# Sliding-window attention and SwiGLU: unit 7's attention-value products and x ahead of unit 8's transpositions and scores in the source

## The chip, the cores and the metric

The kernel runs on one core of a Trainium2 chip. The metric is the device time of one execution in microseconds. A core has five engines with a queue each: TensorE (PE in the profile, with its weight loads as PEld) multiplies matrices, VectorE (DVE) and ScalarE (ACT) do the elementwise work and read TensorE's results from PSUM, GpSimd (POOL) issues the loads here, and SyncE (SP) issues transposing DMAs and the stores.

## The reference

Attention with a causal window of 128 keys and a linear bias per head, over 8 batches, 8 heads, 576 positions and head dimension 64. Its output, as 4608 tokens by 512, is the input of a gated feed-forward network (FFN) with 1536 hidden columns.

```python
scores = scale * np.matmul(q, k.transpose(0, 1, 3, 2))
bias = slopes[:, None, None] * (-np.abs(rel))[None, :, :]
mask = (rel >= 0) & (rel < window)            # window = 128
scores = np.where(mask, scores + bias[None], -1e9)
attn = softmax(scores)                        # over the keys
attn_out = np.matmul(attn, v)

x = attn_out.transpose(0, 2, 1, 3).reshape(B * S, H * D)
g = x @ w_gate
silu = g * (1.0 / (1.0 + np.exp(-g)))
out = (silu * (x @ w_val)) @ w_out
```

## The kernel before

**Units of attention.** A unit is 128 query rows with all 8 heads. Two batches make nine units (`units`, `p` from 0 to 8): four of the first batch, four of the second, and one combined unit (`p == 8`) that holds the last 64 rows of both. There are 36 units. Unit 8 is the first combined one. A unit needs: its k and q transposed (`transposed`, line 198: four products by an identity into the tile `pt`, copied out by ACT for k and by DVE for q; from rank 11 on a transposing DMA on SP in place of it), scores (`scores`, line 243; products `ps` at line 278 or, for units with 128 keys, `psc` at line 313, both with 64 rows of the array per head), the exponentials on ACT (lines 284 and 317, into `ex` and `exc`), the mask on DVE (lines 290 and 321), the attention-value products `av` (`weighted`, line 325, products at line 345, then a reciprocal and `x` on DVE), and x transposed (`x_transposed`, line 358: four products into `px`, copied to `xT` by ACT). Scores of a combined unit are three sets of 128 keys; for unit 8 all three are made at once (`first + together(...)`).

**FFN.** Blocks of 512 tokens. Block 0 takes units 0 to 3, block 1 units 4 to 7, and so on; block 8 takes the combined units. A block makes, for 12 groups of 128 hidden columns, a gate product `pg` and a value product `pv` (line 397, four products each; ACT's tanh into `tt`, DVE's `uu` at line 416 and `hT` at line 427), and then the output product: `project` (line 446, `po` at line 451, twelve products) for block 0, and seven products in place of eight (`strassen`, line 504, products at line 532) for the others, for which DVE makes sums of weights (`weight_sums`, T at lines 475 to 478) and of `hT` (lines 485 to 488).

**Order.** `attention` (line 838) and `ffn` are generators. `everything` (line 937) walks through the FFN's steps, and after each pulls as many steps of the attention as a target says (`n_att < target`), or until the unit that the next block needs is done (`done < ready[blk]`, `ready[1]` being 8). For a unit `i`, `attention` first emits the transpositions and the scores of unit `i + 1`, one yield per step of these, then `weighted(i)`, a yield, `loads_to(i + 7)` and `ahead(i)`, a yield, `x_transposed(i)` and two yields. The value that it yields becomes `done`. What stands in the source is not yet the order on the engines: up to step 60 of the FFN a scheduler arranges TensorE, DVE and ACT from its own estimates, with the source's order as priority; from step 60 on (`FIXED_FROM`) TensorE's order is the source's, while DVE and ACT are still arranged. POOL's loads stand in the source's order throughout.

**Memory for products.** PSUM has 8 banks. The pool `ps_a` (tag "a") has 4, shared by `ps`, `psc`, `pt`, `av`, `px` and the strassen product `p`. The tag "gv" has 3, for `pg` and `pv`. The tag "po" has 1.

Of the kernel before, what the change touches and what calls it, by code (L numbers as in the profile page):

```python
# [39 lines left out]
def slot(h):  # L40

    return 4 * (h // 4) + 2 * (h % 2) + (h % 4) // 2
# [9 lines left out]
def kernel(  # L52
# [141 lines left out]
    def load(rank):  # L194
        load_qk(rank)
        load_v(rank)
# [34 lines left out]
    need = [18 * s + n for s in range(NSUP) for n in (3, 5, 7, 8, 11, 13, 15, 18 if s else 16, 18)]  # L231

    def transpose(n):
        name, rank = order[n]
        if rank < QK_DMA_FROM:
            transposed(name, rank)
            return
        t_ = (natk if name == "k" else natq).pop(rank)
        nc.sync.dma_start_transpose(transposed_home(name, rank), t_.rearrange("p h d -> p (h d)"))
# [3 lines left out]
    def scores(i):  # L243

        s, p = units[i]
        def combined(n):
            return scores_128(s, (3, 7, 8)[n], 8, (s, "c", n), msk[n])

        def together(one, two):
            return [one[0] + two[0]] + one[1:] + two[1:]  # L250

        if p == 8:
            first = combined(0) if s == 0 else []
            return first + together(combined(1), combined(2))
        if p == 7 and s == 0:
            return scores_128(s, p, p, (s, p), reg[:, :, 0:P])
        if p == 7:
            return together(scores_128(s, p, p, (s, p), reg[:, :, 0:P]), combined(0))
        if p == 3:
            return scores_128(s, p, p, (s, p), reg[:, :, 0:P], i < FIRST)  # L260
        ks = (9 * s + p) % NK
        banks = []
        early_tile = i < FIRST
        e = epool.tile([P, H, 256], FP16, name="ex", tag="ex", bufs=4)
        ex[(s, p)] = e

        def products():
            for q4 in range(2):
                two = [ps_a.tile([P, 2, 256], FP32, name="ps", tag="a") for _ in range(2)]
                banks.append(two)  # L270
                for par in range(2 if early_tile else 0):
                    o = 4 * q4 + 2 * par
                    nc.tensor.matmul(two[par], idm, bias[:, o:o + 2, :], start=True, stop=False)
                for j in range(2):
                    pair = 2 * q4 + j
                    for par in range(2):
                        rows = slice(64 * par, 64 * par + 64)
                        nc.tensor.matmul(two[par][:, j, :], kT[rows, ks, pair, :],  # L278
                                         qT[rows, p:p + 2, pair, :], start=(j == 0 and not early_tile),
                                         stop=(j == 1))  # L280

        def act(q4, par):
            o = 4 * q4 + 2 * par
            nc.scalar.activation(e[:, o:o + 2, :], banks[q4][par], AF.Exp, scale=scale)  # L284

        def mul(q4):
            if early_tile:
                return
            o = slice(4 * q4, 4 * q4 + 4)
            nc.vector.tensor_mul(e[:, o, :], e[:, o, :], reg[:, o, :])  # L290

        return [[products], [lambda: act(0, 0)], [lambda: act(0, 1), lambda: mul(0)],
                [lambda: act(1, 0)], [lambda: act(1, 1), lambda: mul(1)]]
# [31 lines left out]
    def weighted(i):  # L325

        s, p = units[i]
        x = xpool.tile([P, H, D], FP16, name="x", tag="x")
        xs[i] = x
        for half in range(2):  # L330
            pool, tag = (ps_f, "gv") if i < FIRST else (ps_a, "a")
            av = pool.tile([P, 4, D + 1], FP32, name="av", tag=tag)
            todo = []
            for j in range(4):
                h = 4 * half + j
                if p == 8:
                    for n, kt in enumerate((3, 7, 8)):
                        todo.append((j, ex[(s, "c", n)][:, slot(h), :], va[9 * s + kt][:, h, :]))
                else:
                    if p not in (0, 4):  # L340
                        todo.append((j, ex[(s, p - 1)][:, slot(h), 128:256],
                                     va[9 * s + p - 1][:, h, :]))
                    todo.append((j, ex[(s, p)][:, slot(h), 0:128], va[9 * s + p][:, h, :]))
            for n, (j, w, val) in enumerate(todo):
                nc.tensor.matmul(av[:, j, :], w, val, start=(n == 0), stop=(n == len(todo) - 1))  # L345
            rec = xpool.tile([P, 4, 1], FP32, name="rec", tag="rec", bufs=4)
            nc.vector.reciprocal(rec, av[:, :, D:D + 1])
            nc.vector.tensor_mul(x[:, 4 * half:4 * half + 4, :], av[:, :, 0:D],  # L348
                                 rec.broadcast_to([P, 4, D]))
# [3 lines left out]
    def place(i):  # L353

        s, p = units[i]
        return (8, s) if p == 8 else (2 * s + p // 4, p % 4)

    def x_transposed(i):
        n, j = place(i)
        if n not in xT:  # L360
            xT[n] = bpool.tile([P, NKB, 512], FP16, name="xT", tag="xTc" if n == 8 else "xT",
                               bufs=1 if n == 8 else 3)
        x = xs.pop(i).rearrange("p h d -> p (h d)")
        dst = xT[n][:, :, j * P:(j + 1) * P]
        if i >= X_DMA_FROM:
            nc.sync.dma_start_transpose(dst, x)
            return
        pool, tag, n = (ps_f, "po", 1) if i < FIRST else (ps_a, "a", 4)
        pt = pool.tile([P, NKB, P], FP16, name="px", tag=tag, bufs=n)
        for kb in range(NKB):  # L370
            nc.tensor.transpose(pt[:, kb, :], x[:, kb * P:(kb + 1) * P], idm if i < FIRST else idm2)  # L371
        if i < FIRST:
            nc.vector.tensor_copy(dst, pt)  # L373
        else:
            nc.scalar.copy(dst, pt)
# [404 lines left out]
    def loads_to(r):  # L780
        nonlocal loaded
        while loaded <= min(r, NR - 1):
            load(loaded)
            loaded += 1

    def transposes_to(n):
        nonlocal done_t
        while done_t < n:
            transpose(done_t)
            done_t += 1  # L790

    def ahead(i):

        n = need[min(i + 4, last)]
        while done_t < n and order[done_t][1] < loaded and order[done_t][1] >= QK_DMA_FROM:
            transposes_to(done_t + 1)

    def run(steps):
        for fs in steps:
            for f in fs:  # L800
                f()
            yield
# [35 lines left out]
    def attention():  # L838

        waiting = []  # L840
        transposes_to(need[FIRST])
        for _ in run(scores(FIRST)):
            yield FIRST
        for i in range(FIRST, last + 1):
            late = i >= LATE
            if i < last:
                transposes_to(need[i + 1])
                for n, _ in enumerate(run(scores(i + 1))):
                    yield i - len(waiting)
                    if n == 2 and late:  # L850
                        weighted(i)
                        yield i - len(waiting)
            if not late or i == last:
                weighted(i)
                yield i
            loads_to(i + 7)
            ahead(i)
            yield i - len(waiting)
            if late and i < X_DMA_FROM:
                if waiting:  # L860
                    x_transposed(waiting.pop(0))
                waiting.append(i)
                yield i
                yield i
                continue
            while waiting:
                x_transposed(waiting.pop(0))
            x_transposed(i)
            yield i
            yield i + 1  # L870
# [40 lines left out]


    att = attention()
    done = n_att = 0
    ready = [4, 8, 13, 17, 22, 26, 31, 35, 36]
# [90 lines left out]
```

## Time and profile before

| | us |
|---|---|
| median of 4 runs (lowest to highest) | 343.99 (343.88 to 344.37) |
| the profiled execution's own time | 343.88 |
| its span, first to last instruction | 342.1 |
| TensorE busy | 329.5 |
| DVE busy | 277.1 |
| ACT busy | 207.0 |
| POOL busy | 109.6 |

The granted TensorE clock is 1.00 in every stretch. By stretch, busy time (us) of TensorE, DVE and ACT:

| stretch | TensorE | DVE | ACT |
|---|---|---|---|
| 40 to 50 | 9.37 | 8.47 | 7.14 |
| 50 to 60 | 9.57 | 6.49 | 6.86 |
| 60 to 70 | 9.98 | 9.78 | 5.03 |
| 70 to 80 | 9.92 | 9.89 | 7.13 |
| 80 to 90 | 9.76 | 9.88 | 5.53 |
| 90 to 100 | 9.34 | 7.75 | 6.34 |
| 200 to 243 | 42.94 | 42.93 | 22.77 |

The span is counted from the first instruction to the last; the time of a run lies a little above it. In an order of time, a line gives the start, the length, the engine, the source line, the operation, output<-input, the shape, how many instructions of that kind follow one another (xN), and in brackets the idle time before it with what ended it. Matmuls are pipelined, so the length of one is longer than the distance to the next: what a product costs is read from one start to the next. The shape "64*128" marks products with 64 rows of the array.

### The profile page before, as it was taken

Reading aid. Unit: us, or ns where it says so; the run is one execution under the profiler, and the core shown is the slowest. Engines: PE = TensorE matmul, PEld = TensorE weight load, DVE = VectorE, ACT = ScalarE, POOL = GpSimd, SP = SyncE. Lnnn points to the kernel's source line nnn. Section 1 sums busy time; section 2 is a strip of 40 time slices with the busy share of each in tenths; the row PEclk is TensorE's granted clock in tenths of the full one; section 3 lists DMA queues with packets and bytes.
Section 4 is the critical chain, followed back from the end, with each engine's and each line's share of the span. In section 5 each row is a group of like instructions: output and inputs, shape, how many; then the busy total and the mean of one; then the engine's idle time right before and its main releaser. Section 6 shows DMA issues by size and latency. Waiting matters only on the chain.

```text
span 342.1 us, 7786 instructions
## 1 busy us (share of the span) xinstructions
PE 329.5 (96%) x2983; PEld 218.2 (64%) x2983; DVE 277.1 (81%) x652; ACT 207.0 (61%) x412; POOL 109.6 (32%) x136
## 2 busy tenths in 40 slices
PE   7999989999999999999999999999999999999995
PEld 3484445444456565565655655666788878888884
DVE  5577886999798769998899999999855975775683
ACT  3758676465666665666655647563477667676640
POOL 8977662648865176833017000000000000000000
PEclk9999999999999999999999999999999999999999
DMA  9999999999999999999949912041101101011014
GB/s 151 167 180 177 166 175 147 82 144 153 158 173 151 161 155 181 162 158 139 193 111 104 176 31 79 15 72 38 63 6 57 63 0 64 19 45 63 0 71 116
DMA packets 160037, 37.37 MB, mean 109 GB/s; under 512 B 147328, under 2 KB 155648, under 8 KB 160000
## 3 DMA queue, kind: packets, MB, share of 16 engines
q0 software_dynamic: 118336, 18.62, 82.1%
q1 hardware_dynamic: 40976, 17.64, 27.1%
q10 hardware_dynamic: 688, 0.62, 0.6%
q8 instruction: 23, 0.38, 0.5%
q14 instruction: 14, 0.11, 0.1%
HBM read 37.91 MB, written 9.44 MB: 138 GB/s over the span
## 4 chain that ended last, share of the span: by engine, by line
PE 75%; DVE 14%; ACT 6%; issue 3%; DMA 1%; ACTq 0%; DVEq 0%
PE po L532 16%; PE pg L397 14%; PE pv L397 14%; PE gX L624 8%; PE av L345 4%; PE gY L624 4%; PE ps L278 3%; PE p L532 2%; PE po L451 2%; DVE hT L427 2%; PE gZ L624 2%; ACT tt L415 2%; ACT ex L284 2%; DVE uu L416 2%; PE px L371 1%
## 5 line engine op out<-in xcount | busy, mean ns | idle before, releaser
L397 PE MATMUL pv<-xT,wv_sb 128*128 128x512 f16 (+2 forms) x320 | 76.5, 358 | 0.6 <-DVE uu L416 0.3
L397 PE MATMUL pg<-xT,wg_sb 128*128 128x512 f16 (+2 forms) x320 | 75.8, 358 | 0.3 <-DVE xT L373 0.2
L415 ACT ACTIVATE tt<-pg 128x512 f16<-128x512 f32 (+2 forms) x70 | 41.3, 590 | 47.7 <-PE pg L397 46.6
L284 ACT ACTIVATE ex<-ps 128x512 f16<-128x512 f32 x96 | 50.0, 606 | 9.8 <-PE ps L278 9.7
L416 DVE SCALAR_TENSOR_TENSOR uu<-tt,pg 128x512 f16<-128x512 f16 (+2 forms) x69 | 45.9, 665 | 11.3 <-ACT tt L415 11.0
L427 DVE TENSOR_TENSOR hT<-uu,pv 128x512 f16<-128x512 f16 (+2 forms) x70 | 46.6, 666 | 3.0 <-PE pv L397 1.3
L185 POOL DMA_DIRECT2D va<-in_v_dram x40 | 34.4, 865 | 37.0 <-PE av L345 31.1
L397 PEld LDWEIGHTS <-wv_sb 128*128 128x128 f16 x320 | 28.4, 98 | 24.9 <-issue 3.0
L532 PEld LDWEIGHTS <-hT 128*128 128x128 f16 x384 | 36.9, 98 | 11.3 <-issue 1.7
L397 PEld LDWEIGHTS <-wg_sb 128*128 128x128 f16 x320 | 28.3, 98 | 23.3 <-issue 2.6
L191 POOL DMA_DIRECT2D qn<-in_q_dram x39 | 33.4, 863 | 19.1 <-DMA va<-in_v_dram 11.8
L191 POOL DMA_DIRECT2D kn<-in_k_dram x39 | 33.3, 858 | 18.0 <-DMA kT<-kn 10.7
L532 PEld LDWEIGHTS <-S 128*128 128x128 f16 x288 | 27.3, 98 | 9.0 <-issue 1.4
L290 DVE TENSOR_TENSOR ex<-ex,m_reg 128x1024 f16<-128x1024 f16 x42 | 28.8, 687 | 3.0 <-ACT ex L284 3.0
L348 DVE TENSOR_TENSOR x<-av,rec 128x256 f16<-128x256 f32 x72 | 28.7, 420 | 0.4
L532 PE MATMUL po<-T,S 128*128 128x256 f16 x192 | 26.6, 273 | 0.6 <-DVE S L487 0.3
L532 PE MATMUL po<-T,hT 128*128 128x256 f16 x192 | 26.0, 273 | 0.1
L676 DVE TENSOR_TENSOR hT<-s,v 128x512 f16<-128x512 f16 x18 | 7.6, 423 | 18.5 <-ACT s L675 18.5
L317 ACT ACTIVATE exc<-psc 128x512 f16<-128x512 f32 x40 | 21.3, 609 | 1.9 <-PE psc L313 1.9
L345 PEld LDWEIGHTS <-ex 128*128 128x128 f16 x384 | 17.4, 97 | 4.6 <-issue 1.1
L345 PE MATMUL av<-va,ex 128*128 128x65 f16 x384 | 19.3, 193 | 0.7 <-ACT ex L284 0.7
L278 PE MATMUL ps<-qT,kT 64*128 64x256 f16 x192 | 16.7, 272 | 0.4 <-DVE qT L223 0.2
(134 smaller groups left out, 535.5 us busy)
## 6 DMA issues: line engine op xcount, KB each, us to landing
out_dram<-osb SPq DMA_DIRECT2D x32, 256.0 KB, 2.5
va<-in_v_dram POOLq DMA_DIRECT2D x32, 128.0 KB, 7.8
qn<-in_q_dram POOLq DMA_DIRECT2D x31, 128.0 KB, 8.0
kn<-in_k_dram POOLq DMA_DIRECT2D x31, 128.0 KB, 8.3
wg_sb<-in_moe_w_gate_dram POOLq DMA_DIRECT2D x6, 256.0 KB, 7.6
wv_sb<-in_moe_w_val_dram POOLq DMA_DIRECT2D x6, 256.0 KB, 8.2
wo_sb<-in_moe_w_out_dram POOLq DMA_DIRECT2D x2, 768.0 KB, 9.5
kn<-in_k_dram POOLq DMA_DIRECT2D x8, 64.0 KB, 7.3
```

The source lines that it names most:

```text
L185: nc.gpsimd.dma_start(va[rank][p0:p1, :, 0:D], src)
L191: nc.gpsimd.dma_start(t_[p0:p1], src)
L284: nc.scalar.activation(e[:, o:o + 2, :], banks[q4][par], AF.Exp, scale=scale)
L290: nc.vector.tensor_mul(e[:, o, :], e[:, o, :], reg[:, o, :])
L345: nc.tensor.matmul(av[:, j, :], w, val, start=(n == 0), stop=(n == len(todo) - 1))
L348: nc.vector.tensor_mul(x[:, 4 * half:4 * half + 4, :], av[:, :, 0:D], rec.broadcast_to([P, 4, D]))
L397: nc.tensor.matmul(ps[:, c0:c1], w[:, kb, ms], xT[n][:, kb, c0:c1], start=(kb == 0 and c0 == 0), stop=(kb == NKB - 1 and c1 == 512), skip_ ...
L415: nc.scalar.activation(tt, pg[:, c0:c1], AF.Tanh, scale=0.5)
L416: nc.vector.scalar_tensor_tensor(out=uu, in0=tt, scalar=one if (n, m) == PIN else 1.0, in1=pg[:, c0:c1], op0=ALU.add, op1=ALU.mult)
L427: nc.vector.tensor_mul(hT[n][:, m, c0:c1], acted[(n, m)][1][:, c0:c1], pv[:, c0:c1])
L532: nc.tensor.matmul(dst, a[:, m, cols], b[:, m, :], start=(start and m == 0), stop=(m == HM - 1), skip_group_check=True)
L624: nc.tensor.matmul(dst[:, i, :], w[:, kb, c0 + i * P:c0 + (i + 1) * P], a[:, kb, :], start=(start and i == 0 and kb == 0), stop=(i == 1 an ...
```

## The change

In the generator `attention` unit 7 gets a branch of its own. It emits `weighted(7)`, a yield, `x_transposed(7)`, a yield, and only then the transpositions and scores of unit 8, the loads, `ahead` and a yield. The calls are the same and are made once each. There are nine yields for the unit where there were ten (six for the scores in both), and from `x_transposed(7)` on they say 8, where before 8 came only with the last. Other units are untouched.

```diff
         for i in range(FIRST, last + 1):
             late = i >= LATE
+            if i == 7:
+                weighted(i)
+                yield i
+                x_transposed(i)
+                yield i + 1
+                transposes_to(need[i + 1])
+                for _ in run(scores(i + 1)):
+                    yield i + 1
+                loads_to(i + 7)
+                ahead(i)
+                yield i + 1
+                continue
             if i < last:
                 transposes_to(need[i + 1])
                 for n, _ in enumerate(run(scores(i + 1))):
```

## The prediction

> **What bounds the kernel now.** I read the page's busy shares and its chain first, then the stretch that the change touches on TensorE in order of time, then VectorE (DVE) and ScalarE (ACT) beside it, then the waits.
>
> ```profile
> PE 329.5 (96%) x2983; PEld 218.2 (64%) x2983; DVE 277.1 (81%) x652; ACT 207.0 (61%) x412; POOL 109.6 (32%) x136
> ...
> PE 75%; DVE 14%; ACT 6%; issue 3%; DMA 1%; ACTq 0%; DVEq 0%
> ```
>
> TensorE is busy for 96% of the span and makes up 75% of the chain. The change adds and removes no operation, so only time in which TensorE does not stream can be won or lost. The stretch from 48 to 79 us in the order of time, TensorE alone (start, length, line, operation, count, idle time before it and its releaser):
>
> ```profile
> 49.24 0.28 PE L371 MATMUL px<-idm,x 128*128 128x128 f16 x2 [0.57 <-DVE x L348]
> ...
> 50.50 0.44 PE L313 MATMUL psc<-qT,kT 64*128 64x128 f16 x9
> 51.13 0.38 PE L313 MATMUL psc<-qT,kT 64*128 64x128 f16 x7 [0.20 <-ACT xT L375]
> 51.44 0.39 PE L451 MATMUL po<-wo_sb,hT 128*128 128x512 f16 x1
> ...
> 56.47 1.02 PE L397 MATMUL pg<-xT,wg_sb 128*128 128x512 f16 x4
> 57.33 1.03 PE L397 MATMUL pv<-xT,wv_sb 128*128 128x512 f16 x4
> ...
> 60.87 0.28 PE L278 MATMUL ps<-qT,kT 64*128 64x256 f16 x2
> 61.15 1.02 PE L397 MATMUL pv<-xT,wv_sb 128*128 128x512 f16 x4
> ...
> 77.69 0.61 PE L278 MATMUL ps<-qT,kT 64*128 64x256 f16 x8
> 78.23 1.04 PE L397 MATMUL pv<-xT,wv_sb 128*128 128x512 f16 x4
> ```
>
> Three things are to be seen. The first gate product (pg) of FFN block 1 starts only at 56.47, because it needs x of unit 7; until then TensorE is filled with unit 8's score products (psc), transpositions (pt) and output products (po), in small pieces. Starting a kind to starting the next, four 512-column products take 0.86 (56.47 to 57.33), eight ps 0.54 (77.69 to 78.23), but two ps 0.28 (60.87 to 61.15): (0.54 - 0.28) / 6 = 0.043 each, and 0.28 - 2 x 0.043 = 0.19 for being a block at all. Entering a block costs another 0.10 (four pg at 76.73, and ps only at 77.69, so 0.96 where 0.86 is due). And the px of unit 6 waits for DVE.
>
> ```profile
> 49.10 0.68 DVE L321 TENSOR_TENSOR exc<-exc,m_reg 128x1024 f16<-128x1024 f16 x1
> ...
> 50.36 0.68 DVE L427 TENSOR_TENSOR hT<-uu,pv 128x512 f16<-128x512 f16 x1
> ...
> 58.16 0.75 DVE L416 SCALAR_TENSOR_TENSOR uu<-tt,one,pg 128x512 f16<-128x512 f16 x1 [1.68 <-ACT tt L415]
> ```
>
> DVE, in order of time: it masks unit 7's exponentials until 49.78, closes block 0 with hT, and idles 1.68 before block 1's first uu, 1.69 after that block's first pg started. From there on it is nearly full (19.67 of 20 us busy between 60 and 80), so a block that starts earlier must find DVE free too.
>
> **The change part by part.** The 24 psc of unit 8 and its transpositions are issued later; the loads and the transposing DMAs that the unit issues (loads_to, ahead) keep their places: in the built order POOL's queue is the same, and SP's is the same until past 100 us, so no load passes a neighbour in its queue. In the built order TensorE now runs: px of unit 6 (2 of 4), 13 av of unit 7, px (2), 3 av, 4 po, 4 px and 8 pt of unit 8 mixed, 1 po, then pg; behind it psc x8, pv, pg, psc x16, pv, pg, pv, pg, pv, 12 pt, pg, 3 pv, ps x8 in one piece, 1 pv, 3 po, 24 av, 4 po, pg, px of unit 8. I lay this on the rows of before. All of it costs the same per product, and what is queued behind the waiting av of unit 7 is all of TensorE: po, px of unit 7 and pg.
>
> Up to the first px at 49.24 nothing differs. The 13 av need the masked exponentials: 49.78 plus 0.06 gives 49.84; 13 at 0.03 (24 av take 0.73) end at 50.24; 2 px and 3 av end at 50.44. The po need block 0's last hT; DVE now does it straight after x of unit 6, so 50.03 to 50.71, and po start at 50.77 (0.33 lost). Four po (0.87), 4 px (0.22), 8 pt (0.45), 1 po (0.22) end at 52.53. Before, pg started 0.95 after the last pair of px (55.52 to 56.47, the ACT copy of x lies between); the last pair now stands at 51.81, so pg starts at 52.76, which is 3.71 earlier.
>
> What was skipped comes back: pg ends 53.62; entry 0.10 and psc x8 0.33 (47.46 to 47.79) give 54.05; pv and pg 55.77; entry and psc x16 (0.56, 112.22 to 112.78) 56.43; pv, pg, pv, pg 59.87. Here DVE is late: uu of the first pair at 52.76+1.69 = 54.45, then hT, mask, T sum, uu, mask, hT, mask and uu at 0.60 to 0.66 each put the third uu's end at 60.13, so the next pv waits 0.33, starting at 60.20 and ending 61.06. Twelve pt (0.67), pg, 3 pv (0.65): 63.24. The ps need the copy of q, which DVE's queue gives at about 63.35; entry and 0.54: 64.04. One pv, 3 po, 24 av, 4 po, pg: 67.37, and the px of unit 8 starts there. Before it starts at 68.73, with 3 pv (0.65) ahead of it that now follow: 68.08. **Gain 0.71.** DVE is further ahead than TensorE there, as the T sums of line 475 moved forward into its idle time; so it does not hold the gain back.
>
> From 67 to 97 the order differs little. Unit 13's ps go as 4 and 4 instead of 4, 2 and 2: one block less (0.19 in itself and 0.10 entry, together 0.29), and its px no longer splits psc from av where 0.24 was waited at 85.74, of which I take half. **Gain 0.41**, bounds 0 and 0.53.
>
> From 97 on TensorE's order is the source's. The rewritten unit yields nine times instead of ten, so all later attention work stands one step earlier against the FFN. In four places the 16 av, which take two banks of the 4-bank pool, now stand ahead of 6 products p, which take one, instead of behind. The trace of before does not show that order. The nearest rows:
>
> ```profile
> 98.91 0.61 PE L278 MATMUL ps<-qT,kT 64*128 64x256 f16 x8
> ...
> 100.33 0.82 PE L532 MATMUL p<-wo_sb,hT 128*128 128x256 f16 x6
> ```
>
> The ps take all four banks and the four exponentials that free them run 99.51 to 101.57, one per 0.5. With av first, p comes at about 100.85 and its bank at 101.1: 0.3. In the other three places only two banks were taken or two groups lie between, so nothing by the same reckoning. Bounds for all four: 0 and 4 x 0.69 = 2.8, since p directly behind ps at 118.36 waits 0.69. I take **0.3 lost**, by the row at the place itself. Everything else after 97 I cost at nothing: between a unit's exponentials and its av, and between its av and its px, stand one or two groups of 0.86 or 0.65, as before, and these cover ACT and DVE; without such cover a wait of 0.3 to 0.7 would show, as at the two places named.
>
> The sum: -0.71 - 0.41 + 0.3 = -0.8. The profiled execution took 343.88 (span 342.1 and 1.78 around it): 343.1 for it; the median of the runs stands 0.11 above it, so 343.2.
>
> The Trainium skill (TensorEngine Tiling (Array Packing), section Key Properties) says that a change of tiling mode drains TensorE. The rows agree that a block has a price, 0.10 in and 0.19 for itself. An estimate from TensorE: Matmul & The Clock Gate, section Single matmul latency, with its fixed 166 ns at each of the two changes, would give 0.33 per block. The built order has 41 such blocks instead of 45, so by that estimate the four fewer are worth 1.3, and by the rows 1.2. In the layouts above the blocks are counted by the rows.
>
> **The rivals.** *More is won (341.5 to 342.4):* the DVE wait at 60 does not come, as DVE reaches the third uu in time, and the waits of 0.66 on exponentials at 95 vanish with an earlier ACT: -0.8 - 0.33 - 0.66 = -1.8, so 342.2. For it speaks DVE's lead; against it that ps x8 still stands directly ahead of 8 av. A limit stands at 2: unit 11's products at 77.69 need a q whose transposition was issued at 68.47 and takes 7.0 to land.
>
> *It is hidden (343.4 to 344.3):* DVE is busy 42.93 of the 43 us from 200 to 243. If it sets the pace there and its new order adds small waits, the 0.8 is given back: 343.9.
>
> *Slower:* the bank wait decides. If the av ahead of p cost 0.69 in all four places, 2.8 is lost against 1.1 won: +1.7, 345.7. It decides from about 0.45 per place, where the sum passes 344.7. For it: p at 118.36 shows that price. Against: only one of the four places follows a full ps x8 closely.
>
> *The move changes nothing on the chip* is excluded by the built order, in which pg of block 1 comes ahead of unit 8's scores.
>
> **How the numbers follow.** Forecast 342.5 to 343.7: 0.50. More won: 0.11. Hidden: 0.15. Slower: 0.24. The likeliest gives 343.2. About 0.2% (0.69 us, so 343.30 and 344.68) is what a measurement of this kernel can tell from no change. Of the forecast's half, about 0.38 lies below 343.30 and 0.12 within; with 0.11 that makes 0.49 faster; 0.12 and 0.15 make 0.27 the same; 0.24 slower. The range for 8 in 10 goes from 342.0, which cuts off less than a tenth, to 345.5, near the slower case's price, which cuts off another tenth; the forecast's own is 342.5 to 343.7.
>
> **What would show it.** Right: pg of block 1 near 52.8, av of unit 7 at 49.8, one ps x8 near 63.5, px of unit 8 near 67.4. Wrong: pg after 54, TensorE waits above 0.5 between 53 and 64, p waiting for exponentials at several places after 97, or a px of unit 8 that comes no earlier in spite of an early pg.

## The result, and the profile after

| | before | after |
|---|---|---|
| median of the runs | 343.96 (59 runs) | 344.83 (37 runs) |
| lowest to highest | 343.61 to 345.36 | 344.49 to 345.29 |
| the profiled execution's own time | 343.88 | 344.87 |
| its span | 342.1 | 343.1 |

After to before: 1.0024, interval 1.0020 to 1.0029. The change makes the kernel slower by 0.87 us; 343.2 was predicted, with 0.24 for slower. The busy shares and the chain on the page of after:

```profile
PE 329.5 (96%) x2983; PEld 218.5 (64%) x2983; DVE 276.9 (81%) x652; ACT 207.7 (61%) x412; POOL 109.6 (32%) x136
...
PE 61%; DVE 26%; ACT 6%; issue 4%; DMA 1%; ACTq 0%; DVEq 0%
```

The work is the same; the chain now runs through DVE for 26% of the span where it was 14%. The groups of the page name the products that wait: the scores `ps` have 1.5 us of idle time ahead of them (0.4 before), 1.0 of it behind x: 0.26 at 142 and 0.74 at 199, as will be seen.

```profile
L278 PE MATMUL ps<-qT,kT 64*128 64x256 f16 x192 | 16.8, 272 | 1.5 <-DVE x L348 1.0
```

The stretch that the change rewrites, TensorE in order of time:

```profile
49.83 0.20 PE L345 MATMUL av<-va,exc 128*128 128x65 f16 x1 [0.25 <-DVE exc L321]
...
50.76 1.04 PE L451 MATMUL po<-wo_sb,hT 128*128 128x512 f16 x4 [0.22 <-DVE hT L427]
...
52.75 1.02 PE L397 MATMUL pg<-xT,wg_sb 128*128 128x512 f16 x4
53.71 0.40 PE L313 MATMUL psc<-qT,kT 64*128 64x128 f16 x8
...
60.34 1.02 PE L397 MATMUL pv<-xT,wv_sb 128*128 128x512 f16 x4 [0.18 <-DVE uu L416]
...
63.47 0.61 PE L278 MATMUL ps<-qT,kT 64*128 64x256 f16 x8
...
67.74 0.28 PE L371 MATMUL px<-idm,x 128*128 128x128 f16 x2 [0.24 <-DVE x L348]
```

The first gate product of block 1 is there at 52.75, not 56.47, and everything up to 63 lies within 0.15 of the layout in the prediction. The loss is elsewhere. To find it, take the n-th gate product (pg) in both traces and the difference of their starts, after minus before: -0.48 at 77 us, -0.60 at 96, -0.70 from 109 to 141, -0.57 at 192, then +0.56 at 201 and at 210, and +1.08 from 228 to 239. The change is ahead until 192 and loses 1.65 us in the 47 us behind it: 1.13 by 201 and 0.52 more by 228. (Single values shift by about 0.65 where a neighbouring group has changed sides with a pg, such as +1.20 at 204; a step counts where the values stay.)

TensorE there in the change, and DVE beside it:

```profile
194.67 0.65 PE L345 MATMUL av<-va,ex 128*128 128x65 f16 x16
195.15 0.82 PE L532 MATMUL p<-wo_sb,hT 128*128 128x256 f16 x6
195.80 1.03 PE L397 MATMUL pv<-xT,wv_sb 128*128 128x512 f16 x4
196.67 0.82 PE L532 MATMUL po<-T,S 128*128 128x256 f16 x6
197.42 0.62 PE L278 MATMUL ps<-qT,kT 64*128 64x256 f16 x5
198.77 0.39 PE L278 MATMUL ps<-qT,kT 64*128 64x256 f16 x3 [0.74 <-DVE x L348]
199.09 1.04 PE L397 MATMUL pg<-xT,wg_sb 128*128 128x512 f16 x4
```

```profile
195.55 0.69 DVE L321 TENSOR_TENSOR exc<-exc,m_reg 128x1024 f16<-128x1024 f16 x1
196.15 0.18 DVE L347 RECIPROCAL rec<-av 128x4 f32<-128x4 f32 x1
196.36 0.42 DVE L348 TENSOR_TENSOR x<-av,rec 128x256 f16<-128x256 f32 x1
196.71 0.68 DVE L416 SCALAR_TENSOR_TENSOR uu<-tt,pg 128x512 f16<-128x512 f16 x1
197.30 0.42 DVE L537 SCALAR_TENSOR_TENSOR osb<-p,p1s 128x256 f32<-128x256 f32 x1
197.63 0.17 DVE L347 RECIPROCAL rec<-av 128x4 f32<-128x4 f32 x1
197.72 0.66 DVE L427 TENSOR_TENSOR hT<-uu,pv 128x512 f16<-128x512 f16 x1
198.30 0.42 DVE L348 TENSOR_TENSOR x<-av,rec 128x256 f16<-128x256 f32 x1
199.20 0.43 DVE L601 TENSOR_TENSOR kT<-wg_sb,kT 128x512 f16<-128x512 f16 x1 [0.48 <-PE ps L278]
```

And TensorE, then DVE, at the same place in before:

```profile
195.24 0.82 PE L532 MATMUL p<-wo_sb,hT 128*128 128x256 f16 x6
195.89 0.65 PE L345 MATMUL av<-va,ex 128*128 128x65 f16 x16
196.37 1.03 PE L397 MATMUL pv<-xT,wv_sb 128*128 128x512 f16 x4
197.24 0.82 PE L532 MATMUL po<-T,S 128*128 128x256 f16 x6
197.89 1.03 PE L397 MATMUL pg<-xT,wg_sb 128*128 128x512 f16 x4
198.85 0.61 PE L278 MATMUL ps<-qT,kT 64*128 64x256 f16 x8
199.40 1.04 PE L397 MATMUL pv<-xT,wv_sb 128*128 128x512 f16 x4
```

```profile
196.41 0.68 DVE L416 SCALAR_TENSOR_TENSOR uu<-tt,pg 128x512 f16<-128x512 f16 x1
197.01 0.42 DVE L537 SCALAR_TENSOR_TENSOR osb<-p,p1s 128x256 f32<-128x256 f32 x1
197.34 0.24 DVE L347 RECIPROCAL rec<-av 128x4 f32<-128x4 f32 x2
197.55 0.76 DVE L348 TENSOR_TENSOR x<-av,rec 128x256 f16<-128x256 f32 x2
198.23 0.68 DVE L427 TENSOR_TENSOR hT<-uu,pv 128x512 f16<-128x512 f16 x1
199.65 0.69 DVE L416 SCALAR_TENSOR_TENSOR uu<-tt,pg 128x512 f16<-128x512 f16 x1 [0.74 <-ACT tt L415]
```

Eight `ps` need all four banks of the pool "a". At 197.42 two of them are still held: one by `p`, until `osb` (line 537) has read it at 197.72, and one by the second `av` tile, until the second x has. The bank of the first `av` tile is free, as the first x ended at 196.36 + 0.42 = 196.78. The `ps` fill a pair of banks in turns, so the fifth needs the third bank and the sixth the fourth: the fifth starts at 197.77, just behind `osb`, and then TensorE stops until the second x ends at 198.30 + 0.42 = 198.72. From the first `ps` to the product behind them 1.67 us go by (197.42 to 199.09) where before takes 0.55 (198.85 to 199.40): 1.12 is lost here, nearly all of the 1.13 by 201. DVE is then itself 0.48 idle behind `ps`, since its next operation writes over the kT that `ps` reads (before has 0.74 of idle time there too, behind ACT's tt). In before one more group of 0.86, a pg, stands ahead of `ps`, and DVE does both x in one piece (197.55 to 198.31): all banks are free at 198.85. So the change asks for all four banks 1.4 us earlier (197.42 for 198.85) and gets x 0.4 later (198.72 for 198.31). Two more such places appeared, `ps` at 142 (0.26 behind x) and `psc` at 217 (0.35 behind osb).

The Trainium skill, PSUM — Partial Sum Buffer, section Engine vs sequencer instructions, says that VectorE's queue is strictly first in, first out and that matmuls start in program order. These lines agree: the second x, whose av products were issued by 195.15, ahead of the first x, stands 1.94 us behind that one (196.36 to 198.30) because uu, osb and hT are queued between, and pg, which needs none of these banks, waits behind `ps`.

### The profile page after: what moved, and what is told of

Its sections match the earlier page's. It is cut to its first block, busy times and chain, and to the rows that moved or that the text cites. A ratio compares the mean times of both kernels' runs of the same rounds, so it can differ in the third digit from the quotient of the medians.

```text
span 343.1 us, 7785 instructions
## 1 busy us (share of the span) xinstructions
PE 329.5 (96%) x2983; PEld 218.5 (64%) x2983; DVE 276.9 (81%) x652; ACT 207.7 (61%) x412; POOL 109.6 (32%) x136
## 4 chain that ended last, share of the span: by engine, by line
PE 61%; DVE 26%; ACT 6%; issue 4%; DMA 1%; ACTq 0%; DVEq 0%
PE po L532 14%; PE pg L397 10%; PE pv L397 10%; PE gX L624 8%; DVE uu L416 5%; DVE hT L427 5%; PE gY L624 4%; PE av L345 3%; DVE ex L290 2%; ACT ex L284 2%; DVE x L348 2%; PE po L451 2%; PE ps L278 2%; PE p L532 2%; PE gZ L624 2%
```

## Experiments

Theory: the move itself wins; what loses is the yield that went missing (nine for ten), which puts all later attention one group earlier against the FFN. Where DVE has no slack (34.93 of 35 us busy from 205 to 240 before) a group of score products then meets banks that DVE has not yet freed. (At 198 itself DVE is not full by its busy time: 12.15 of 13 us from 192 to 205 before, with the 0.74 idle shown above. What is late there is the second x in its queue; DVE is full behind that place.) The last two columns of this table are the difference of the same gate product to before, at 192 us and at 239 us, in the profiled executions; their difference is what was lost in between.

| kernel | median | before beside it | ratio, interval | at 192 | at 239 |
|---|---|---|---|---|---|
| the change | 344.83 | 343.96 | 1.0020 to 1.0029 | -0.57 | +1.08 |
| e1, tenth yield | 343.63 | 344.06 | 0.9979 to 0.9997 | +0.17 | +0.16 |
| e2, nine yields only | 345.46 | 344.06 | 1.0027 to 1.0052 | +0.36 | +1.66 |
| e3, x first | 345.17 | 344.06 | 1.0020 to 1.0045 | -0.59 | +1.55 |
| e5, e1 and e3 | 345.29 | 344.06 | 1.0023 to 1.0048 | +1.26 | +1.63 |
| e7, yield back at 17 | 343.41 | 343.99 | 0.9968 to 0.9992 | -0.46 | -0.47 |
| e8, yield back at 28 | 343.60 | 343.99 | 0.9980 to 0.9998 | -0.58 | -0.57 |
| e11, one out at 28 | 345.00 | 343.90 | 1.0022 to 1.0047 | +0.13 | +1.47 |
| e12, yield back at 30 | 345.04 | 343.90 | 1.0016 to 1.0040 | +0.56 | +2.17 |
| e13, out at 28, back at 30 | 345.12 | 344.09 | 1.0018 to 1.0040 | +0.20 | +1.47 |
| e14, change but 28 to 30 | 343.85 | 344.09 | 0.9965 to 1.0005 | -0.57 | +0.15 |

**The two halves of the change apart.** e1 adds a tenth yield to the new branch, so that later attention stands as in before:

```diff
                 loads_to(i + 7)
                 ahead(i)
                 yield i + 1
+                yield i + 1
                 continue
```

> The change with a tenth yield given back to unit 7, so that all later attention work stands at the same FFN step as before; TensorE's order is then the changed one up to unit 9's scores and the old one from about 80 us on. Theory (the move itself wins, the missing yield loses): 343.2 to 343.6, 0.4 to 0.8 under before, with no wait of scores on x of DVE in 140 to 220. Rival (the move itself loses, through the arrangement of DVE that it brings): 344.5 to 345.2, as the change.

e2 is the kernel before, with one yield of unit 7 left out and nothing moved:

```diff
             while waiting:
                 x_transposed(waiting.pop(0))
             x_transposed(i)
-            yield i
+            if i != 7:
+                yield i
             yield i + 1
```

> The kernel before with one yield of unit 7 left out and nothing moved: TensorE's order is the old one up to about 85 us and mostly that of the change behind it. Theory: the loss alone, 1.3 to 1.8 above before, 345.3 to 345.8. Rival (the move itself loses): 343.8 to 344.2, as before.

The move without the shift wins 0.43 (343.63, just above the 343.2 to 343.6 that its theory gave). In the profile its run starts 0.41 late (at 43 us, ahead of anything changed), is at +0.17 by 96 us, and stays there to the end: 0.24 won and kept. The shift without the move costs 1.40, with the waits of the change at 142, 198 and 217 (0.26, 0.51 and 0.35) and no other new one behind 97 us. By the medians the two halves add up: -0.43 + 1.40 = 0.97, where the change costs 0.87. By the traces they do not do so in every stretch: at 141 us e1 is 0.24 ahead of its own start and e2 0.25 behind, while the change is 0.70 ahead. So what the move wins early on depends on the shift as well, and e1 is not the best that can be had of it; e7 below is better.

**DVE's order mended.** e3 is the change, with rec and x given priority in DVE's arrangement for the late units; TensorE's order is that of the change. e5 is the same on e1.

```diff
-            nc.vector.reciprocal(rec, av[:, :, D:D + 1])
-            nc.vector.tensor_mul(x[:, 4 * half:4 * half + 4, :], av[:, :, 0:D],
-                                 rec.broadcast_to([P, 4, D]))
+            with tc.high_priority() if i >= LATE else ExitStack():
+                nc.vector.reciprocal(rec, av[:, :, D:D + 1])
+                nc.vector.tensor_mul(x[:, 4 * half:4 * half + 4, :], av[:, :, 0:D],
+                                     rec.broadcast_to([P, 4, D]))
```

> The change with the reciprocals and x of units from 13 on at a higher priority, so that DVE does them earlier; TensorE's order is that of the change. Theory (scores wait for PSUM banks that av holds until a late x): the waits at 142.6 and 198.8 us go, 0.8 to 1.5 is won, 343.4 to 344.1. Rival (DVE is full there, and what is put back becomes the next wait): within 0.4 of the change, 344.4 to 345.2.

> Both: the tenth yield given back and x at a higher priority. Theory: the tenth yield leaves little for the priority to win, 343.0 to 343.6. Rival (DVE's order matters as such): 0.5 or more away from the kernel with the tenth yield alone, on either side.

The waits on x vanished as meant, and it did not help: e3 is no faster than the change (0.34 above it, 0.24 when each is held against the kernel before beside it, with intervals that overlap), and e5 is 1.66 slower than e1. TensorE's longest wait in e3 (its lines are numbered one higher):

```profile
228.23 1.02 PE L398 MATMUL pv<-xT,wv_sb 128*128 128x512 f16 x4 [1.11 <-DVE uu L417]
```

and in e5:

```profile
142.83 0.39 PE L533 MATMUL po<-T,S 128*128 128x256 f16 x2 [1.12 <-DVE S L488]
```

What x gained, uu and the sums S lost, and these feed TensorE too. Until 215 us the priority had won (e3 stands at 0.00 there, the change at +0.56); the wait on uu at 228 took that back. The theory's expected gain fell; its rival, that DVE is full and whatever is put back becomes the next wait, held.

**The yield given back, later and later.** e7 is the change with one extra yield at unit 17, e8 at unit 28, e12 at unit 30:

```diff
             ahead(i)
             yield i - len(waiting)
+            if i == 17:
+                yield i - len(waiting)
             if late and i < X_DMA_FROM:
```

> The change with the missing yield given back in unit 17 (about 115 us) in place of never. TensorE's order is that of the change up to there and that of the kernel before from there on. Theory (the time is lost at the scores at 141, 198 and 217 us, and only by the shifted order): 343.2 to 343.7, 0.4 to 0.8 under before. Rival (the lead at 115 us is work put off, not won): 344.0 to 344.5.

> The same with the yield given back in unit 28 (about 205 us), behind the waits at 141 and 198 us and ahead of that at 217. Theory: those two stay and the third goes, 344.2 to 344.7, between the kernel that has the yield back at unit 17 and the change. Rival (the loss lies elsewhere): within 0.2 of either of these.

> The change with one yield given back two units later than before (at unit 30, about 205 us): the shifted order holds from 97 us through the wait at 198 and is that of before from there on. If the waits at 198 carry the loss, the time is near the change's, 344.4 to 344.8; if those at 217 do, near the kernel with the yield given back at unit 28, 343.5 to 343.9. By the lead of the gate products (from -0.57 at 191 us to +0.56 at 209 to 215, and +1.08 at 228 to 239) about two thirds belong to 198, so 344.3.

e7, with the shift between 97 and about 120 us alone, beats both kernels: 343.41, ratio 0.9980. e8 keeps the shift up to about 193 us, and with it the wait at 142, and is still 0.39 below before. Its expectation was missed for two reasons. It took the yield at unit 28 for one at 205 us, behind the wait at 198; in the trace it acts from 193 on, ahead of that wait, which is gone. And it counted on a price for 142, where before has a wait of its own, on S (0.32 at 142.26). The difference does rise there, from -0.71 at 140 to -0.11, but it is back at -0.58 at 192, in pieces too small to show as waits: 0.1 net. Its rival, within 0.2 of e7, held (0.19). e12, with before's order only from about 205 us on, gets nothing back: 345.04, above the 344.3 expected. So the loss is made, for the most part, by what stands between 193 and 205 us.

**One place alone.** e11 is the kernel before with one yield left out at unit 28: identical to before up to 193 us. e13 also gives it back at unit 30, so that TensorE's order differs from before's in four neighbouring groups between 193 and 203 us and nowhere else. e14 is the opposite: the change, with those four groups as in before.

```diff
             ahead(i)
-            yield i - len(waiting)
+            if i != 28:
+                yield i - len(waiting)
+            if i == 30:
+                yield i - len(waiting)
             if late and i < X_DMA_FROM:
```

(e11 has the first two added lines alone; e14 has 30 and 28 exchanged, on the change.) DVE and ACT are arranged anew in each of them.

> The kernel before with one yield of unit 28 left out: nothing else is touched, so unit 7 is as before, and TensorE's order is that of before up to about 193 us and that of the change from there to the end of attention. Theory (what the change loses, it loses between 192 and 240 us, where DVE has no slack and the scores at 198 and 217 need the banks that av and p still hold): waits at about 198 and 217 of 0.3 to 0.5 each behind x and osb, and a time 1.0 to 1.6 above before, 345.0 to 345.5, as with the yield left out at unit 7 (+1.40). Rival (the loss needs what was shifted between 97 and 192, or DVE's queue as the change left it): within 0.4 of before, 343.6 to 344.4.

> The kernel before with one yield left out at unit 28 and given back at unit 30: TensorE's order differs from before's in four places between about 193 and 203 us alone (one psc, one av, one ps and one av block each a group earlier), and nowhere else. Theory (the one place where the scores meet the banks that av still holds until x, at 198, carries the loss): +0.8 to +1.3 above before, 344.7 to 345.3, and a wait of about 0.5 behind x at 198. Rival (198 and 217 share it, as the lead of the gate products suggested): +0.4 to +0.7. Second rival (a late start there is caught up within 20 us, since the order behind it is that of before): within 0.3.

> The change with one yield given back at unit 28 and taken out again at unit 30: the shifted order everywhere from 97 us to the end of attention, but for the same four places between 193 and 203 us, which are as in before. If 198 alone carries the loss, the move's gain comes back in full although the order at 142 and 217 is the shifted one: 343.4 to 343.8. If 217 has a price of its own (the wait of 0.35 behind osb), 343.9 to 344.3. If the loss belongs to the shift as a whole, near the change, 344.6 to 344.9.

e11 runs at a constant +0.13 to before from 56 to 192 us, and at +1.47 from 228 us on, with waits of 0.55 at 199 behind x and 0.35 at 218 behind osb, as its theory expected. e13, with the order of before again from 203 us, costs as much: +1.03. TensorE in e13, in order of time:

```profile
197.44 0.82 PE L532 MATMUL po<-T,S 128*128 128x256 f16 x6
198.19 0.50 PE L278 MATMUL ps<-qT,kT 64*128 64x256 f16 x5
199.22 0.39 PE L278 MATMUL ps<-qT,kT 64*128 64x256 f16 x3 [0.54 <-DVE x L348]
199.54 1.04 PE L397 MATMUL pg<-xT,wg_sb 128*128 128x512 f16 x4
...
218.49 0.39 PE L532 MATMUL po<-T,S 128*128 128x256 f16 x2 [0.66 <-DVE S L487]
```

The wait at 199 is that of the change, and the eight `ps` with it take 1.35 (198.19 to 199.54) where before takes 0.55: 0.80 is lost at the place itself. The wait at 218 is new, although TensorE's order there is that of before. DVE has come out of the first place later and is busy 19.93 of 20 us from 205 to 225, so it has nothing to catch up with. But its order is not that of before either: this S stands behind both x at 218.01, in before between the two, at 216.28. How much of the second wait is lateness and how much is this other order was not tried apart. In e14 the gain is mostly back: 343.85, 0.24 below before beside it, between what its first two cases expected, its interval reaching 1.0005. It keeps a wait of 0.28 behind osb at 216, and its profiled execution loses 0.72 between 192 and 239 against e8's 0.01; by the medians its gain is 0.15 less than e8's (0.24 and 0.39, each against the kernel before beside it). So 198 carries most of the loss, 1.11 between the change (+0.87) and e14 (-0.24), and the shifted order at 217 a smaller part, 0.15 by medians and up to 0.7 by the profile; more closely it was not measured.

**DVE relieved.** e9 is before and e10 the change, both without DVE's multiplication by the mask for units behind unit 13 and for the later 128-key units. Without the mask they do not compute the reference's attention, and serve for their times alone:

```diff
-            if early_tile:
+            if early_tile or i > LATE:
                 return
...
-                [lambda: act(1), lambda: early_tile or nc.vector.tensor_mul(e, e, m)]]
+                [lambda: act(1), lambda: early_tile or s > 1 or nc.vector.tensor_mul(e, e, m)]]
```

> The kernel before without the mask multiplications on DVE of units from 14 on (combined and 128-key units from the third pair of batches on), some 20 us less of DVE's work at an unchanged TensorE order. Both theories: 343.0 to 344.1; it is the base of the next run.

> The change without the same mask multiplications. Theory (the shifted order loses because DVE is full there, so that x comes late): the waits at 142, 198 and 217 us go, and it is 0.3 to 0.9 under the kernel before without those masks. Rival (the shifted order costs by its own spacing of PSUM banks, whatever DVE does): 0.5 to 1.2 above it.

e9 took 342.73, a little under what was expected, and e10 342.49, five runs each: with DVE relieved the change is no slower than its counterpart, where it was 0.87 slower. Whether it is faster is not settled, as their runs overlap (342.49 to 342.90 and 342.10 to 342.93). The waits at 142, 198 and 217 are gone: from 120 to 270 us TensorE in e10 has no idle time above 0.15, at the same order as in the change, and DVE is busy 10.12 of 13 us from 192 to 205 (11.70 in the change). The rival, 0.5 to 1.2 above, fell. The gain falls short of the theory's 0.3 to 0.9, since e10 still loses 0.40 between 191 and 227 (its difference to e9 goes from -0.64 to -0.24). DVE is 19.63 of 20 us busy from 205 to 225 even there.

## Why the prediction was wrong

- **First stretch (gain 0.71).** The layout held: av at 49.83 (49.84 predicted), po 50.76 (50.77), pg 52.75 (52.76), psc 53.71, pv behind uu 60.34 (60.20), ps 63.47 (about 63.4). At its end the px of unit 8 came at 67.74, not 67.37: the pv behind uu had come 0.14 late, and px waits 0.24 for x, which the layout did not have, because it took DVE to be ahead there. 68.08 - 67.74 = 0.34 won instead of 0.71: the term came out at about half. (In its sum, 63.35, 0.10 and 0.54 make 63.99 and not 64.04; that changes nothing here.)
- **67 to 97 (gain 0.41).** From -0.48 at 77 to -0.60 at 96: the two terms together gave 0.60 by 96 us, of 1.12 predicted. Whether the four fewer blocks of 64-row products were worth what the rows said was not tried apart.
- **Sixteen av ahead of p (0.3 lost).** At the place itself 0.32 of TensorE's time went by beyond what the av cost (99.72 to 100.53 where they take 0.49), as taken, and the difference goes from -0.60 at 98 to -0.29 at 101. The 0.69 at 118 stands in both traces. What the prediction did not price is that the shift also wins at one place: in before `po` waits for ACT's p5s at 107.53, 0.42 behind the end of pv, and in the change the 16 av fill that gap. The difference is -0.70 at 109, so no net loss is left.
- Up to 141 us the sum was therefore -0.70 where -0.8 was predicted. That it comes so close is luck: the two gains came to 0.34 and 0.26 in place of 0.71 and 0.41, and 0.41 that nobody had counted was won at 107. Still, the versions that keep before's order behind it hold what they had won to the end: e7 is 0.58 faster than before.
- **The step that failed: "Everything else after 97 I cost at nothing".** Its cover was counted in TensorE's groups, one or two of 0.86 or 0.65 between av and px. But the next claim on what av holds is not px: it is the scores, which need all four banks of "a", and the cover that counts is DVE's queue, in which uu, osb and hT stood between the two x. From 192 to 239 the shift cost 1.65 in the profile of the change and 1.30 in that of e2 (1.40 by e2's medians, over the whole run); in e13 four groups alone cost 1.03.
- **Rivals.** *Hidden* came closest: small waits from DVE's new order, and DVE busy throughout 200 to 243. But it priced them at what had been won, and the largest loss stands just ahead of that stretch, where one late x costs 1.12 though DVE is not full; behind it a full DVE made up none of it. *Slower* had the right resource, the banks of "a" held behind av, and the wrong instruction: it priced p at four places and looked no further than the group that changed sides. Its 345.7 was too high by 0.9. *More won* did not come: the wait on uu at 60 is there (0.18), and so is the one on exponentials at 94.

The parts that keep a reservation: why DVE's arrangement split the two x when the av came earlier is not shown; how much of the loss behind 203 us is DVE's lateness and how much its other order stays open; and the share of 217 is known only roughly.

## What to carry to other kernels

When a move also changes the number of steps that a generator yields, the two are separate changes: pad the steps so that everything behind keeps its place, measure the move alone, and then the shift alone. Where a second engine is full or nearly so, a group of products that is shifted by one place is covered only if that engine's queue frees its banks by then, so the check has to list every claim on the shared pool, the widest first (here eight `ps` for four banks), and not only the pair of groups that changed sides. Giving one consumer priority on a full engine moves the wait and can cost more than it saves.

## What the runs showed of the hardware

- One hand-over that TensorE waited 0.54 us for cost the whole kernel 1.03 (e13): 0.80 at the place, and part of the rest some 20 us later, where TensorE waited 0.66 at 218 for the same DVE.
- Profiled executions differ by up to 0.4 us before anything that was changed: the same gate product at 43 us stands at +0.41 in e1, +0.23 in e7, +0.21 in e13 and at 0.00 in the change. Differences of a few tenths are therefore read from where they arise in a trace, and not from the end of one execution.
- A transposing DMA can land late in a single execution: e12's profiled one waited 1.05 for it at 88.81 and took 345.89, its median 345.04.
